# A linear-attention and FFT-convolution kernel: the filter loaded second, the angles in thirds, the last rows in merged transfers, and a new order of the work

## The chip, the cores and the metric

The kernel runs on one core of one Trainium2 chip. The metric is the device time of one execution in microseconds (us). Three runs of the kernel before gave a median of 219.78 us (219.63 to 219.86). One more execution was taken with the profiler.

## The reference: what is computed

For 8 batches, 8 heads, 576 positions and 64 values per head, all in float32:

```python
kv = np.einsum('bhsd,bhse->bhde', k, v)
out = np.einsum('bhsd,bhde->bhse', q, kv)
rms = np.sqrt(np.mean(out * out, axis=-1, keepdims=True) + 1e-06)
x = out / rms * g_norm            # heads put side by side: (8, 576, 512)
proj = x @ w_proj                 # x1, x2, x3: 512 columns each
X2, H = rfft(x2, axis=1), rfft(filter_fft, axis=0)
y = x1 * irfft(X2 * H, axis=1) * x3
return y @ w_out                  # (8, 576, 512)
```

## The kernel before, in words

**Stages of one batch.** The names are those of the steps in the table ORDER (L20); a step is written `name.batch`.

- Loads: `Lk`, `Lv`, `Lq` (whole or in halves a and b) fetch k, v, q as bf16 through POOL's DMA queue (L136 to L146). There are two buffers of each, so batch b overwrites batch b-2. `Lw1`, `Lw2`, `Lw3` fetch the three parts of w_proj, `Lwo` fetches w_out, `Lf` the filter.
- `K` multiplies k by v on PE (L377), `eK` copies the product to `kvblk`. q is transposed on PE (`T0`, `T1`, L416, copied by `eT..`) for batches 0 and 1 and by a DMA transpose on SP (`Qt`, L407) for the others; behind each `Qt` stands a small POOL copy (L408), which makes POOL wait for the transpose.
- `O` multiplies q by `kvblk` (L447); `sq` squares on ACT (L457); `R` sums on PE (L454); `rs` is the reciprocal root on ACT (L468); `ob` or `ov` copies the product (ACT or DVE); `x` multiplies both on DVE (L489).
- Gates: `Ga` and `Gb` (L631) are x by parts one and three of w_proj, 8 matmuls for each of four column blocks; `x1`/`xv` copies the one, `g` multiplies by the other on DVE (L639).
- The convolution: x is folded (`eo`, `fa`, `fr` on DVE), multiplied by part two of w_proj (`rrM`, `rrT`, `abM`, `abT`, L529 to L549), copied (`err`, `eab`, `eT`, L553), transformed (`F0`, `F1t`, `F1`, `F2c`, `F2`), multiplied by the filter's transform (`M0`, `M1`, `M2` on DVE, L606 and L621), summed (`A` on POOL or `Av` on DVE, L612), transformed back (`I`, `Io`, L661), copied to `ar` (`ea`, `oa` on ACT, `ev`, `ov` on DVE, L665), recombined on DVE (`vB`, `w`) and multiplied by the gates (`fin`, or `f0`, `f1` by halves, L683).
- Output: `U0`, `U2`, `U4` multiply by w_out (L716, L729) and `ot` copies and stores through SP's queue (L723, L736). The last batch has `V0` to `V3` (one bank each, L754), copies `va`/`vv` (L760), and stores `d..` of 32 rows each (L765): `dsCI` from SP, `dgCI` from POOL, `daCI` from ACT, for block group C and quarter I.

**The start.** Angles (`An`, L226) are made on DVE and turned to sines and cosines on ACT in one piece; PE transposes them into tables (`Tb0` to `Tb2`). The filter is folded (`Ff0` to `Ff2`, L315) and transformed (`H0` to `H2`, L332 and L335; copies L343 to L348).

**What sets the order.** ORDER is written by hand or by a search; each engine runs its instructions in the order in which the steps stand there, and waits for others through semaphores. A third number in a word (`T0.0.22`) puts that many filler matmuls on zeros (L112) ahead of the step. PSUM is four pairs of banks. `take` gives a step a pair, or one bank: before, one bank came from a pair with its other bank in use, if there was one. A transfer's end is counted by one of eight semaphore lanes for SP and ACT together (DMAHW0 to 7) and eight for POOL (DMASW0 to 7); a transfer waits for the one before it on its lane.

Of the kernel before, what the change touches and what calls it, by code (L numbers as in the profile page):

```python
# [19 lines left out]
ORDER = """Zi.0 Z.0 Zt.0 Lqa.0 Zd.0 An.0 Zf.0 Act.0 Lva.0 T0.0.22 eTv0.0 Tb1.0 Lka.0 Lvb.0 Tb2.0 Ka.0 eKva.0 Tb0.0 Lqb.0 O01.0.3  # L20
sq1.0 T1.0.3 R1.0.1 Lkb.0 ob1.0 eTv1.0 Lf.0 sq0.0 Kb.0 Lqa.1 eKvb.0 rs1.0 ov0.0 O23.0.4 R0.0 sq2.0 rs0.0 ov2.0 R2.0.2
sq3.0 ov3.0 Ff2.0 R3.0 rs3.0 rs2.0 Ff0.0 Lw1.0 Ff1.0 Lk.1 x.0 T0.1 eo.0 fr.0 eTv0.1 Lv.1 Lw3.0 Lqb.1 Ga0.0 Ga1.0 xv0.0
H0.0 H1.0 fa1.0 HN0.0 xv1.0 H2.0 K.1 Lw2.0 HN1.0 Lv.2 eK.1 Ga3.0 Gb1.0 fa0.0 T1.1 g1.0 eTa1.1 x13.0 Lkb.2 Gb3.0 rrM.0
rrT.0 g3.0 verr.0 O01.1 Lq.2 sq1.1 abM.0 F0.0 ov1.1 sq0.1 abT.0.1 ov0.1 eab.0 O23.1 F2c.0 eT.0 F2.0 sq2.1 M0.0 ob2.1
Gb0.0 M2.0 g0.0 sq3.1 F1t.0 Lka.2 Lqb.3 Lqa.3 A0.0 Qt.2 F1.0 ob3.1 R1.1 R3.1 Ga2.0 rs1.1 rs3.1 M1.0 R0.1 K.2 x12.0
rs0.1 R2.1 rs2.1 Gb2.0 Av1.0 eK.2 x.1 Io23.0 oa23.0 g2.0 Lk.3 I01.0 Io01.0 Lva.3 ea01.0 eo.1 I23.0 Lvb.3 O01.2 Lwo.0
oa01.0 Ga3.1 ea23.0 fa0.1 fa1.1 Qt.3 sq1.2 vB23.0 fr.1 ob1.2 Ga2.1 x13.1 sq0.2 x12.1 Lk.4 abM.1 ob0.2 eab.1 abT.1
O23.2 eT.1 vB01.0 sq2.2 w.0 ob2.2 rrM.1 rrT.1 F2c.1 Gb2.1 F2.1 err.1 fin.0 g2.1 sq3.2 Ga0.1 ob3.2 F0.1 x10.1 M2.1 R1.2
R2.2 rs1.2 Gb3.1 R3.2 rs2.2 F1t.1 F1.1 Lqa.4 Lq.5 M0.1 rs3.2 R0.2 K.3 g3.1 Ga1.1 rs0.2 M1.1 U0.0 eK.3 x11.1 x0.2 x1.2
Av1.1 ot0.0 O23.3 sq2.3 Gb0.1 g0.1 A0.1 ob2.3 eo.2 sq3.3 Gb1.1 I23.1 ob3.3 ea23.1 Ga0.2 Io23.1 g1.1 fa0.2 I01.1 x10.2  # L30
fa1.2 oa23.1 ev01.1 Io01.1 abT.2 O01.3 oa01.1 eT.2 fr.2 Lv.4 sq1.3 sq0.3 abM.2 ob1.3 eab.2 Ga3.2 vB.1 x13.2 rrM.2
ob0.3 R3.3 w.1 K.4 fin.1 F1t.2 rs3.3 F1.2 rrT.2 eK.4 Gb3.2 err.2 Lqb.4 M1.2 R0.3 rs0.3 Gb0.2 R2.3 Qt.4 g3.2 F0.2 g0.2
A1.2 R1.3 rs2.3 rs1.3 U4.1 Ga2.2 Ga1.2 x12.2 Qt.5 M0.2 x11.2 O23.4 F2c.2 x.3 F2.2 sq2.4 ob2.4 sq3.4 ob3.4 Lk.5 eo.3
U2.0 Gb1.2 fa.3 M2.2 U0.1 ot2.0 g1.2 Lk.6 R2.4 ot0.1 abT.3 Lva.5 Lq.6 eT.3 ov4r.1 Gb2.2 Av0.2 I01.2 rs2.4 Io23.2
Io01.2 g2.2 Lvb.5 ea01.2 I23.2 abM.3 oa23.2 fr.3 rrM.3 ev23.2 oa01.2 eab.3 vB.2 rrT.3 O01.4 w.2 F1t.3 err.3 sq1.4 F1.3
ob1.4 Lv.6 sq0.4 U2.1 ob0.4 Ga3.3 F0.3 M1.3 fin.2 A1.3 ot2.1 x13.3 R3.4 Ga2.3 rs3.4 M0.3 x12.3 Gb3.3 K.5 g3.3 eK.5
F2c.3 F2.3 R1.4 Gb2.3 R0.4 A0.3 rs1.4 M2.3 g2.3 I23.3 x1.4 rs0.4 ea23.3 I01.3 ea01.3 x0.4 eo.4 Ga0.3 O23.5 U0.2 sq3.5
ob3.5 xv0.3 fa0.4 sq2.5 ot0.2 ov2.5 fa1.4 Ga1.3 Io23.3 oa23.3 fr.4 Gb0.3 x11.3 abT.4 g0.3 Io01.3 veT.4 K.6 oa01.3
O01.5 eK.6 sq1.5 sq0.5 vB23.3 Gb1.3 ob1.5 vB01.3 abM.4 g1.3 ob0.5 rrM.4 rrT.4 eab.4 w.3 F1t.4 R1.5 Lk.7 f001.3 f101.3
err.4 f023.3 f123.3 R3.5 F1.4 Ga2.4 rs3.5 F0.4 rs1.5 R0.5 x12.4 M1.4 Ga1.4 R2.5 rs0.5 U2.2 x11.4 U4a.3 rs2.5 Qt.6 M0.4  # L40
O23.6 x.5 F2c.4 F2.4 ot2.2 M2.4 sq3.6 Gb1.4 ob3.6 g1.4 A1.4 sq2.6 U4b.3 Ga3.4 A0.4 ot4.3 ob2.6 I23.4 x13.4 eo.5 fr.5
Gb3.4 Io23.4 ea23.4 g3.4 Io01.4 oa23.4 vB23.4 w023.4 Ga0.4 I01.4 oa01.4 Gb2.4 ea01.4 g2.4 rrM.5 x10.4 w123.4 O01.6
rrT.5 sq1.6 vB01.4 U0.3 ov1.6 w001.4 err.5 Gb0.4 fa.5 abT.5 sq0.6 ot0.3 ob0.6 w101.4 R3.6 R2.6 g0.4 veT.5 rs3.6 F0.5
abM.5 rs2.6 Ga2.5 R1.6 f123.4 M0.5 f001.4 f023.4 Lv.7 Lq.7 eab.5 f101.4 x12.5 R0.6 rs0.6 Gb2.5 rs1.6 F1t.5 x1.6 K.7
F2c.5 F2.5 F1.5 Qt.7 A0.5 g2.5 U2.3 eK.7 M2.5 Ga3.5 ot2.3 O23.7 sq2.7 sq3.7 M1.5 xv3.5 Gb3.5 Ga0.5 Av1.5 ob3.7 g3.5
eo1.6 x0.6 eo0.6 x10.5 fa0.6 ob2.7 Ga1.5 Io01.5 Io23.5 I23.5 x11.5 oa23.5 Gb0.5 oa01.5 I01.5 ea01.5 fa1.6 abM.6 ea23.5
U0.4 g0.5 vB01.5 abT.6 fr0.6 eab.6 vB23.5 w001.5 ot0.4 w101.5 Gb1.5 fr1.6 O01.7 eT.6 w023.5 sq0.7 g1.5 ob0.7 F1t.6
w123.5 F1.6 Ga3.6 x13.6 rrM.6 F2c.6 M1.6 sq1.7 rrT.6 R3.7 ob1.7 F2.6 Gb3.6 err.6 rs3.7 fin.5 A1.6 M2.6 g3.6 Ga0.6 F0.6
Ga1.6 R1.7 x10.6 x11.6 Gb1.6 M0.6 rs1.7 Gb0.6 R0.7 Ga2.6 g1.6 R2.7 rs0.7 U0.5 g0.6 A0.6 x0.7 rs2.7 x1.7 xv2.6 I23.6
ot0.5 ea23.6 I01.6 eo.7 Ga1.7 Io01.6 ea01.6 oa01.6 Gb2.6 x11.7 Io23.6 fa.7 oa23.6 abM.7 g2.6 Ga0.7 fr.7 abT.7 eab.7  # L50
eT.7 x10.7 rrM.7 rrT.7 F2c.7 F1t.7 vB.6 F2.7 w.6 F1.7 U2.5 err.7 fin.6 M2.7 M1.7 A1.7 F0.7 ot2.5 M0.7 U0.6 Gb0.7 ot0.6
U2.4 Av0.7 g0.7 Gb1.7 I23.7 ot2.4 I01.7 g1.7 ea01.7 U4a.5 U4b.5 ea23.7 Io01.7 Io23.7 oa01.7 vB01.7 oa23.7 vB23.7 Ga2.7
w001.7 f001.7 Gb2.7 Ga3.7 ot4.5 Gb3.7 x12.7 x13.7 g2.7 g3.7 U2.6 w023.7 f023.7 U4a.7 w123.7 U4b.7 w101.7 ot2.6 va4.7
V0.7 da42.7 da40.7 dg41.7 f101.7 f123.7 dg43.7 V3.7 va3.7 da32.7 vv0.7 V1.7 dg03.7 ds30.7 V2.7 da33.7 da00.7 vv1.7
vv2.7 ds11.7 dg31.7 da02.7 ds13.7 dg01.7 ds23.7 dg12.7 dg10.7 dg22.7 da20.7 da21.7"""
# [3 lines left out]
def kernel(  # L59
# [165 lines left out]
    @one  # L225
    def An(b):  # L226

        ang = work.tile([P, 2, 3, TH], FP32, name="ang", tag="tpw1")
        a_, r_ = ang[:, 0], ang[:, 1]
        for c in range(3):  # L230
            vec.tensor_scalar_mul(out=a_[:, c], in0=tmp['tv'], scalar1=kcol[:, c:c + 1])
        vec.tensor_scalar(out=r_, in0=a_, scalar1=0.5 / S, scalar2=MAGIC, op0=ALU.mult, op1=ALU.add)
        vec.tensor_scalar(out=r_, in0=r_, scalar1=MAGIC, scalar2=-2.0 * S, op0=ALU.subtract, op1=ALU.mult)
        vec.tensor_tensor(out=r_, in0=r_, in1=a_, op=ALU.add)
        act.activation(out=IV[:, 1:6:2], in_=r_, func=AF.Sin, scale=W0)
        act.activation(out=a_, in_=r_, func=AF.Abs)
        for h, n in ((0, 2), (1, 1)):
            act.activation(out=IV[:, 4 * h:4 * h + 2 * n - 1:2], in_=a_[:, 2 * h:2 * h + n], func=AF.Sin, scale=cosb[:, 2 + h:3 + h], bias=cosb[:, h:h + 1])
# [228 lines left out]
    def e_rs(b, j):  # L467
        act.activation(out=halves(rstd()[:, j]), in_=tmp['r', b, j][:, :, 0:TH], func=AF.Abs_reciprocal_sqrt, scale=1.0 / D, bias=bias_eps)  # L468
# [294 lines left out]
    def V_out(b, key, i, q):  # L763
        rows = o_rows(b - 1 + i // 2, (NB - 2, NB - 1, 0, 1)[i]) if key == 4 else o_rows(b, 2 * (b % 2) + 4 * key + i)
        q.dma_start(out=rows, in_=tmp['ot', b, key][32 * i:32 * i + 32])  # L765
# [51 lines left out]
```

## Time and profile before

| what | value |
|---|---|
| median of three runs | 219.78 us |
| the profiled execution's own time | 221.13 us |
| its span | 219.3 us |
| PE, DVE, ACT, POOL busy | 92%, 84%, 67%, 30% |
| instructions | 4987 |
| filler matmuls asked for in ORDER | 36 |
| HBM read, written | 33.69 MB, 9.44 MB |

PE is TensorE's matmuls and PEld its weight loads, DVE is VectorE, ACT ScalarE, POOL GpSimd, SP SyncE; a q behind a name is the engine's queue, in which DMA issues and waits are seen. Rows of instructions give the start, the length, the engine, the line, what is written from what, how many, and in brackets the idle time before them with what ended it. Rows of groups give busy time and mean ns, then idle time and what ended it. Line numbers are those of the kernel before.

### The profile page before, as it was taken

To read this page: it belongs to the slowest core of one execution; us is meant where nothing else is said; L and a number is where in the kernel's file an instruction comes from. 1 tells how busy PE (TensorE), PEld (TensorE's weight loads), DVE (VectorE), ACT (ScalarE), POOL (GpSimd) and SP (SyncE) were. 2 spreads that over 40 slices of the span, in tenths; PEclk is the share of its full clock that TensorE was granted. 3 is DMA by queue.
4 is the path that set the end of the run, shared out by engine and by line. 5 is a ranking of instruction groups with operands and counts; after the bars stand their busy time and mean duration, and the time that the engine had idled before them with its cause. 6 is when DMAs were issued, how large, how long until landed. Compare 5 with 4: busy or idle time off the path is not lost.

```text
span 219.3 us, 4987 instructions
## 1 busy us (share of the span) xinstructions
PE 200.9 (92%) x2017; PEld 120.7 (55%) x2041; DVE 184.4 (84%) x284; ACT 146.8 (67%) x227; POOL 66.0 (30%) x72
## 2 busy tenths in 40 slices
...
GB/s 48 165 214 200 208 205 206 204 208 162 208 202 147 166 135 83 137 241 257 243 111 138 73 4 160 198 152 54 96 0 99 0 6 94 0 193 111 13 184 175
DMA packets 37146, 30.16 MB, mean 137 GB/s; under 512 B 16162, under 2 KB 32546, under 8 KB 37122
## 3 DMA queue, kind: packets, MB, share of 16 engines
...
q1 hardware_dynamic: 19394, 11.93, 23.4%
q10 hardware_dynamic: 384, 0.52, 0.9%
...
HBM read 33.69 MB, written 9.44 MB: 197 GB/s over the span
## 4 chain that ended last, share of the span: by engine, by line
PE 79%; DVE 6%; ACT 5%; issue 4%; POOL 2%; POOLq 0%; DVEq 0%; ACTq 0%
PE ps L631 27%; PE ps L716 11%; PE ps L543 6%; PE ps L661 4%; PE ps L454 4%; PE ps L529 3%; PE ps L549 3%; PE ps L377 2%; PE ps L447 2%; PE ps L536 2%; PE ps L587 2%; PE ps L573 2%; POOL out_dram L765 2%; PE ps L332 1%; PE ps L112 1%
## 5 line engine op out<-in xcount | busy, mean ns | idle before, releaser
L631 PE MATMUL ps<-x,wp 128*128 128x288 bf16 x512 | 71.2, 286 | 0.4 <-DVE HH L348 0.2
L631 PEld LDWEIGHTS <-wp 128*128 128x128 bf16 x512 | 48.9, 98 | 18.2 <-issue 2.5
L612 POOL TENSOR_TENSOR Y<-tpw 97x1024 bf16<-97x1024 f32 (+1 forms) x11 | 29.1, 2648 | 64.4 <-DVE tpw L606 64.3
L606 DVE TENSOR_TENSOR tpw<-ps,HH 97x2048 f32<-97x2048 f32 (+1 forms) x16 | 36.4, 2288 | 2.5 <-PE ps L587 1.3
L639 DVE TENSOR_TENSOR g<-ps,x 128x576 bf16<-128x576 f32 x32 | 24.0, 752 | 4.2 <-PE ps L631 2.2
L468 ACT ACTIVATE rstd<-ps,bias_eps 128x576 bf16<-128x576 f32 x32 | 23.1, 742 | 5.6 <-PE ps L454 5.4
L716 PE MATMUL ps<-wo,yg 128*128 128x512 bf16 x107 | 26.2, 379 | 0.4 <-ACT x L637 0.2
L553 ACT CAST x<-ps 128x1024 bf16<-128x1024 f32 (+1 forms) x21 | 18.6, 893 | 8.4 <-PE ps L543 4.7
L457 ACT ACTIVATE sq<-ps 128x576 bf16<-128x576 f32 x32 | 20.7, 659 | 4.7 <-PE ps L447 4.6
L720 ACT COPY ot<-ps 128x1024 f32<-128x1024 f32 x14 | 14.2, 1017 | 13.8 <-PE ps L716 12.1
L637 ACT CAST x<-ps 128x576 bf16<-128x576 f32 x27 | 17.5, 647 | 7.5 <-PE ps L631 5.6
L665 ACT CAST ar<-ps 128x576 bf16<-128x576 f32 x30 | 18.1, 645 | 6.4 <-PE ps L662 6.2
L464 ACT ACTIVATE o<-ps,g_col 128x576 bf16<-128x576 f32 x25 | 18.7, 753 | 0.0
L408 POOL COPY one__101<-qT 1x2 bf16<-1x2 bf16 x6 | 4.0, 670 | 46.7 <-DMA qT<-qb 46.7
L716 PEld LDWEIGHTS <-yg 128*128 128x128 bf16 x112 | 10.8, 98 | 12.3 <-issue 0.9
L661 PE MATMUL ps<-IV,Y 128*128 128x192 bf16 x128 | 15.9, 245 | 0.1
L543 PE MATMUL ps<-wp,ab 128*128 128x512 bf16 x59 | 14.9, 379 | 0.3
L662 PE MATMUL ps<-IV,Y 97*128 97x96 bf16 x64 | 13.2, 207 | 1.4 <-DVE Y L612 1.4
L140 POOL DMA_DIRECT2D qb<-in_q_dram x12 | 8.9, 745 | 12.6 <-PE ps L416 9.9
L454 PE MATMUL ps<-sq,ind 128*128 128x288 bf16 x64 | 12.3, 286 | 0.2 <-issue 0.2
L112 PE MATMUL ps<-nil,ind 128*128 128x512 bf16 x34 | 10.7, 441 | 2.0 <-DVE ind L193 1.6
L489 DVE TENSOR_TENSOR x<-o,rstd 128x1152 bf16<-128x1152 bf16 (+1 forms) x12 | 11.9, 1008 | 0.6 <-ACT rstd L468 0.6
...
## 6 DMA issues: line engine op xcount, KB each, us to landing
...
vb<-in_v_dram POOLq DMA_DIRECT2D x5, 576.0 KB, 17.2
...
kb<-in_k_dram POOLq DMA_DIRECT2D x4, 288.0 KB, 13.6
```

The source lines that it names most:

```text
L454: nc.tensor.matmul(r2[:, h, 0:TH], ind, sq()[:, j, h * TH:(h + 1) * TH], start=True, stop=True)
L457: act.activation(out=halves(sq()[:, j]), in_=tmp['o', b, j][:, :, 0:TH], func=AF.Square)
L464: act.activation(out=halves(osb()[:, j]), in_=i_, func=AF.Copy, scale=g_col)
L468: act.activation(out=halves(rstd()[:, j]), in_=tmp['r', b, j][:, :, 0:TH], func=AF.Abs_reciprocal_sqrt, scale=1.0 / D, bias=bias_eps)
L543: nc.tensor.matmul(pp[:, h], abt()[:, j, 2 * h * P:(2 * h + 1) * P], w2(j), start=(j == 0), stop=(j == NDC - 1))
L553: act.copy(out=o_(), in_=tmp[key, b])
L606: vec.tensor_mul(out=t_[:n], in0=xp[:n].unsqueeze(1).to_broadcast([n, 2, 2, DM]), in1=two)
L612: op(out=Yt()[:n, 2 * g:2 * g + 2], in0=t_[:n, ::-1, 0], in1=t_[:n, ::-1, 1])
L631: nc.tensor.matmul(pp[:, h, 0:TH], w_, x[:, j, h * TH:(h + 1) * TH], start=(j == 0), stop=(j == NDC - 1))
L639: vec.tensor_mul(out=halves(g13t()[:, dc]), in0=pp[:, :, 0:TH], in1=x1)
L661: nc.tensor.matmul(pp[:, i, 0:SB], Y[:, 2 * g + h, cs], IV[:, 2 * g + h, 0:SB], start=(g == 1), stop=(g == 2))
L716: nc.tensor.matmul(pp[:, cc], ygt(b)[:, dc, b % 2 * 64 + c * P:b % 2 * 64 + (c + 1) * P], wo[:, dc], start=(dc == 0), stop=(dc == NDC - 1))
```

## The change

1. **Loads.** The filter (`Lf`) stands second, behind the first half of q and ahead of the rest of batch 0; `Lw3` now precedes `Lw1`. Whole loads of q are mostly split into halves.
2. **Filter.** Folding and the first part of its transform (`H1`) come ahead of batch 0's O, `H0` and `H2` ahead of its gates. The folded filter lies in the output buffer yg instead of the work buffer that the angles use.
3. **Angles** are made in thirds (`An2`, `An1`, `An0`): three DVE operations and three ACT operations each.
4. **`take`**: one bank comes from a half-used pair only if no pair is free.
5. **Last rows**: each block of the last batch is stored by two transfers instead of four, over 1 to 3 groups of 32 rows; ACT issues none of them.
6. **`Qh`**: the POOL copy is a step of its own and stands behind every second transpose.
7. `rs` has its small bias as an immediate value.
8. **ORDER** is written anew: 37 fillers, five more `ar` copies on DVE, ten sums on POOL instead of eleven.

The loads at the start of POOL's queue, before; `qb`, `vb`, `kb` are q, v, k with buffer numbers (74, 72, 70 for batch 0; 75 for q of batch 1), `fn` is the filter, `wp` w_proj:

```order
L140 DMA qb_74<-in_q_dram 96x4x384
L144 DMA vb_72<-in_v_dram 128x2x576
L144 DMA kb_70<-in_k_dram 128x2x576
L144 DMA vb_72<-in_v_dram 128x2x576
L140 DMA qb_74<-in_q_dram 96x4x384
L144 DMA kb_70<-in_k_dram 128x2x576
L301 DMA fn<-in_moe_filter_fft_dram 96x3072
L140 DMA qb_75<-in_q_dram 96x4x384
L152 DMA wp<-in_moe_w_proj_dram 128x4x512
```

And after:

```order
L140 DMA qb_74<-in_q_dram 96x4x384
L307 DMA fn<-in_moe_filter_fft_dram 96x3072
L140 DMA qb_74<-in_q_dram 96x4x384
L144 DMA vb_72<-in_v_dram 128x2x576
L144 DMA kb_70<-in_k_dram 128x2x576
L144 DMA vb_72<-in_v_dram 128x2x576
L144 DMA kb_70<-in_k_dram 128x2x576
L152 DMA wp<-in_moe_w_proj_dram 128x4x512
```

The filter has moved ahead of five transfers of batch 0, and the first part of w_proj ahead of batch 1's q.

ACT's queue behind the tables, before; `ff` is the folded filter and `hu` a copy of its transform, `sq` and `rstd` belong to batch 0's norm:

```order
L457 ACTIVATE sq<-ps_68 128x576
L464 ACTIVATE o<-ps_68,g_col 128x576
L457 ACTIVATE sq<-ps_67 128x576
L468 ACTIVATE rstd<-ps_66,bias_eps 128x576
L457 ACTIVATE sq<-ps_69 128x576
L468 ACTIVATE rstd<-ps_66,bias_eps 128x576
L457 ACTIVATE sq<-ps_68 128x576
L468 ACTIVATE rstd<-ps_69,bias_eps 128x576
L468 ACTIVATE rstd<-ps_67,bias_eps 128x576
L317 CAST ff<-ps_68 128x1024
L317 CAST ff<-ps_66 128x1024
L343 ACTIVATE hu<-ps_66,cf 97x1024
```

And after, where the folded filter is written to `yg`:

```order
L323 CAST yg<-ps_67 128x1024
L323 CAST yg<-ps_68 128x1024
L429 COPY qT<-ps_69 128x1152
L349 ACTIVATE hu<-ps_68,cf 128x1024
L466 ACTIVATE sq<-ps_67 128x576
L466 ACTIVATE sq<-ps_66 128x576
L389 CAST kvblk_78<-ps_69 128x2x64
L389 CAST kvblk_78<-ps_69 64x2x64 x2
L466 ACTIVATE sq<-ps_69 128x576
L466 ACTIVATE sq<-ps_68 128x576
L477 ACTIVATE rstd<-ps_66 128x576
```

The filter's copies have moved from behind the norm to ahead of it, with one of the three transform copies and the copy of K's second half between them.

The end of SP's queue, before, with the semaphores that each issue waits for; `ot` holds output blocks, `vb`, `kb`, `sq` serve as output buffers of the last batch:

```order
L723 DMA out_dram<-ot 32x2x512 [waits DMAHW2_49]
L723 DMA out_dram<-ot 32x2x512 [waits DMAHW4_49]
L736 DMA out_dram<-ot 32x512 [waits DMAHW7_49,Activation_49]
L736 DMA out_dram<-ot 32x512 [waits DMAHW1_49]
L736 DMA out_dram<-ot 32x512 [waits DMAHW3_49]
L736 DMA out_dram<-ot 32x512 [waits DMAHW5_49]
L723 DMA out_dram<-ot 32x2x512 [waits DMAHW7_49,Activation_49]
L723 DMA out_dram<-ot 32x2x512 [waits DMAHW0_49]
L723 DMA out_dram<-ot 32x2x512 [waits DMAHW1_49]
L723 DMA out_dram<-ot 32x2x512 [waits DMAHW2_49]
L765 DMA out_dram<-vb_73 32x512 [waits DMASW7_49,DMAHW3_49,DMASW4_49,Activation_49]
L765 DMA out_dram<-kb_71 32x512 [waits DMAHW4_49,DMASW3_49,DVE_49]
```

And after:

```order
L732 DMA out_dram<-ot 32x2x512 [waits DMAHW7_49,Activation_49]
L732 DMA out_dram<-ot 32x2x512 [waits DMAHW0_49]
L732 DMA out_dram<-ot 32x2x512 [waits DMAHW1_49]
L732 DMA out_dram<-ot 32x2x512 [waits DMAHW2_49]
L781 DMA out_dram<-vb_72 2x32x512 [waits DMAHW3_49,DMASW4_49,Activation_49]
L781 DMA out_dram<-kb_71 32x512 [waits DMAHW4_49,DMASW7_49,DVE_49]
L781 DMA out_dram<-kb_71 3x32x512 [waits DMAHW5_49]
L781 DMA out_dram<-vb_73 32x512 [waits DMAHW6_49,DMASW6_49]
L781 DMA out_dram<-sq 2x32x512 [waits DMAHW7_49,DVE_49]
L781 DMA out_dram<-sq 2x32x512 [waits DMAHW0_49]
L781 DMA out_dram<-kb_70 3x32x512 [waits DMAHW1_49,DMASW5_49,Activation_49]
```

The lanes follow each other by one now, since SP alone uses them there, and five of the last seven issues carry two or three groups of 32 rows, listed with the group as outermost dimension.

The diff, cut; of ORDER its first and last lines:

```diff
-ORDER = """Zi.0 Z.0 Zt.0 Lqa.0 Zd.0 An.0 Zf.0 Act.0 Lva.0 T0.0.22 eTv0.0 Tb1.0 Lka.0 Lvb.0 Tb2.0 Ka.0 eKva.0 Tb0.0 Lqb.0 O01.0.3
+ORDER = """Z.0 Lqa.0 Zi.0 Lf.0 Zt.0 An2.0 An1.0 An0.0 Zd.0 Act.0 Zf.0 Zr.0 T0.0.18 Tb2.0 Lqb.0 Tb0.0 eTv0.0 Lva.0 Tb1.0.3 Ff0.0
...
-vv2.7 ds11.7 dg31.7 da02.7 ds13.7 dg01.7 ds23.7 dg12.7 dg10.7 dg22.7 da20.7 da21.7"""
+ds10.7 U4b.7 dg21.7 V0b.7 vv4.7 va0.7 ds30.7 dg00.7 ds40.7 ds41.7 ds01.7"""
...
-        if n == 1 and odd:
+        if n == 1 and odd and all(max(seen[2 * i], seen[2 * i + 1]) >= TAKEN for i in range(4)):
...
+        vec.tensor_scalar_mul(out=kturn, in0=kcol, scalar1=0.5 / S)
...
+    def angles(c):
+
+        if 'ang' not in tmp:
+            tmp['ang'] = work.tile([P, 2, 3, TH], FP32, name="ang", tag="tpw1")
+        a_, r_ = (tmp['ang'][:, i, c] for i in range(2))
+        h = c // 2
+        vec.tensor_scalar(out=a_, in0=tmp['tv'], scalar1=kturn[:, c:c + 1], scalar2=MAGIC, op0=ALU.mult, op1=ALU.add)
+        vec.tensor_scalar(out=r_, in0=a_, scalar1=MAGIC, scalar2=-2.0 * S, op0=ALU.subtract, op1=ALU.mult)
+        vec.scalar_tensor_tensor(out=a_, in0=tmp['tv'], scalar=kcol[:, c:c + 1], in1=r_, op0=ALU.mult, op1=ALU.add)
+        act.activation(out=IV[:, 2 * c + 1], in_=a_, func=AF.Sin, scale=W0)
+        act.activation(out=r_, in_=a_, func=AF.Abs)
+        act.activation(out=IV[:, 2 * c], in_=r_, func=AF.Sin, scale=cosb[:, 2 + h:3 + h], bias=cosb[:, h:h + 1])
...
-            tmp['ff'] = work.tile([P, 3, 2, DM], BF16, name="ff", tag="tpw1")
+            tmp['ff'] = yg4().rearrange("p a j s -> p (a j s)")[:, 0:6 * DM].rearrange("p (a i d) -> p a i d", a=3, i=2)
...
+    @one
+    def Qh(b):
         nc.gpsimd.tensor_copy(out=one_, in_=qT(b)[0:1, 0, 0:2])
...
-        act.activation(out=halves(rstd()[:, j]), in_=tmp['r', b, j][:, :, 0:TH], func=AF.Abs_reciprocal_sqrt, scale=1.0 / D, bias=bias_eps)
+        act.activation(out=halves(rstd()[:, j]), in_=tmp['r', b, j][:, :, 0:TH], func=AF.Abs_reciprocal_sqrt, scale=1.0 / D, bias=1e-6)
...
     def V_out(b, key, i, q):
-        rows = o_rows(b - 1 + i // 2, (NB - 2, NB - 1, 0, 1)[i]) if key == 4 else o_rows(b, 2 * (b % 2) + 4 * key + i)
-        q.dma_start(out=rows, in_=tmp['ot', b, key][32 * i:32 * i + 32])
+        if key == 4:
+            bb, blk, i0, n = b - 1 + i, (NB - 2, 0)[i], 2 * i, 2
+        else:
+            x0 = 2 * (b % 2) + 4 * key
+            cut = 3 - x0 % 3 if x0 % 3 else 3
+            i0, n = ((0, cut), (cut, 4 - cut))[i]
+            bb, blk = b, x0 + i0
+        rows = bass.AP(tensor=out.tensor, offset=out.offset + (bb * S + t_of(blk)) * DM, ap=[[2 * DM, n], [6 * DM, 32], [1, DM]])
+        q.dma_start(out=rows, in_=tmp['ot', b, key][32 * i0:32 * (i0 + n)])
...
-        for i in range(4):
+        for i in range(2):
             for e, q_ in (("s", nc.sync), ("g", nc.gpsimd), ("a", nc.scalar)):
                 step["d%s%d%d" % (e, c, i)] = lambda b, c=c, i=i, q_=q_: V_out(b, c, i, q_)
```

90 lines of the change are left out of this document (41 added, 49 removed).

## The prediction

> **What bounds the kernel now.** I read the page first, then the stretches, the timelines of PE, SP and the copies, the waits and the DMA view.
>
> ```profile
> span 219.3 us, 4987 instructions
> PE 200.9 (92%) x2017; PEld 120.7 (55%) x2041; DVE 184.4 (84%) x284; ACT 146.8 (67%) x227; POOL 66.0 (30%) x72
> 40.00:50.00 10.00, 9.16 (x141) 5.74 (x141) 9.20 (x7) 8.20 (x14) 4.04 (x4) 1.00 1.23 207
> 205.00:210.00 5.00, 4.17 (x20) 1.67 (x18) 1.67 (x5) 1.97 (x3) 1.06 (x2) 1.00 0.25 54
> 210.00:215.00 5.00, 0.00 (x0) 0.00 (x0) 1.62 (x3) 0.00 (x0) 2.95 (x6) 0.76 0.81 222
> 215.00:219.30 4.30, 0.00 (x0) 0.00 (x0) 0.00 (x0) 0.00 (x0) 0.00 (x0) 0.50 0.51 153
> ```
>
> In the stretches the columns after the length are PE, PEld, DVE, ACT, POOL, then clock, DMA share and GB/s. PE is busy for 92% of the span, so the middle is PE's, with DVE close behind. After 209.2 PE does nothing: the last 10 us belong to transfers. Time can come from three places: PE's start, PE's stalls in the middle, and the end.
>
> The end first, by PE's and SP's timelines and SP's waits:
>
> ```profile
> 205.55 3.62 PE L754 MATMUL ps<-wo,yg 128*128 128x512 bf16 x16
> 200.56 11.25 SPq L736 DMA_DIRECT2D out_dram<-ot  x4
> 211.91 2.95 SPq L723 DMA_DIRECT2D out_dram<-ot  x4
> 216.70 0.36 SPq L765 DMA_DIRECT2D out_dram<-vb  x1
> SPq L736 <- DMA out_dram<-sq: 9.0, 2, 8.7
> ```
>
> The last matmul ends at 205.55 + 3.62 = 209.17; the span ends 10.15 us later. SP stood for 8.7 us in one L736 issue, since its semaphore lane was held by a row transfer that ACT issues late, and the 512 KB of batch 6 left only at 211.91. The last issue is at 216.70.
>
> **The end, part by part.** The changed order issues nothing from ACT there, so SP's lanes follow each other and that wait goes. What is late next is the merged transfer itself. V_out now lists the rows as 3 or 2 blocks x 32 rows, with the block dimension outermost, against 96 or 64 partitions. One transfer of the old kernel has such a short outermost dimension: g_col, listed as 2 x 64 against 128 partitions. The DMA view from 0 to 5 us, where g_col is SP's only transfer; ACT's queue on the page (each row packets, MB, share); and the costs beside them:
>
> ```profile
> q1 hardware_dynamic: 130, 0.00, 1.1%
> q10 hardware_dynamic: 384, 0.52, 0.9%
> g_col<-in_g_norm_dram SPq DMA_DIRECT2D x1, 0.5 KB
> L199 SPq DMA_DIRECT2D g_col<-in_g_norm_dram x1: 724/724/724, 0.7 to 0.7; - x1
> out_dram<-kb SPq DMA_DIRECT2D x2, 64.0 KB, 2.1
> 216.80:217.10 0.30, 0.00 (x0) 0.00 (x0) 0.00 (x0) 0.00 (x0) 0.00 (x0) 0.50 0.58 191
> ```
>
> ACT's queue carried 8 transfers of 32 rows: 384 = 8 x (32 + 16), one closing packet from each of 16 engines. g_col left 130 = 128 + 2: two engines. I take a merged transfer to run on 3 or 2 engines, so each of them carries 32 rows of 2 KB, 65.5 KB, where the old 32-row transfer gives each engine two rows.
>
> [...]
>
> Price of one: the load stretch 40 to 50 moves 207 GB/s of bf16 out of twice that in fp32, 414 / 16 = 25.9 GB/s an engine, so 2.5 us; the stretch 216.8 to 217.1 moves 191 / 16 / 0.58 = 20.6 GB/s per busy engine, so 3.2 us. I take 2.7, nearer the fast row, since a narrow transfer has its engine almost alone. SP issues five of them (one of V2, V1, V0 each, two of U4), between two wide ones. On the same engines they run one after the other: 13.5 us (12.5 to 16), and 0.4 for the wide ones' rows.
>
> When the first starts, from the rows of the copies:
>
> ```profile
> 202.41 1.58 DVE L639 TENSOR_TENSOR g<-ps,x 128x576 bf16<-128x576 f32 x2
> 205.62 0.83 DVE L683 TENSOR_TENSOR yg<-w,g 128x576 bf16<-128x576 bf16 x2
> 205.80 0.59 ACT L760 COPY sq<-ps 128x512 f32<-128x512 f32 x1
> ```
>
> After the last gate (call its end t) DVE needs 0.79 for g2 and 0.42 for the product, so with the semaphores between them V3's second half starts at about t+1.4; V3 and V2 are done by t+2.5, their two copies on ACT by t+3.3. PE has 20 matmuls of 0.22 behind the gate (3.62 / 16) and waits about 0.75 for DVE: it ends at t+5.05. So the first narrow issue stands at T - 1.65, T being the last matmul's end. A wide 64 KB lands 2.1 after its issue, 0.2 of it data, so 1.9 is fixed; before, the end came 219.3 - (216.70 + 2.1) = 0.5 after the last landing. End = T - 1.65 + 1.9 + 13.5 + 0.4 + 0.5 = T + 14.65, against T + 10.15: **+4.5** (+3.5 to +7.0). PE's wait of 0.75 stands for one of some 0.35 between the last rows of before: **+0.4**. POOL's two narrow transfers go beside these; on the same engines each would add 2.7, which the upper end covers.
>
> **The start.** PE's rows, of which everything useful counts:
>
> ```profile
> 24.08 2.12 PE L631 MATMUL ps<-x,wp 128*128 128x288 bf16 x16
> 31.29 0.78 PE L377 MATMUL ps<-vb,kb 64*64 64x64 bf16 x72
> 36.27 1.03 PE L529 MATMUL ps<-wp,rr 128*128 128x512 bf16 x3
> 38.15 1.90 PE L543 MATMUL ps<-wp,ab 128*128 128x512 bf16 x8
> L152 POOL DMA_DIRECT2D wp<-in_moe_w_proj_dram x1: 747/747/747, 15.4 to 15.4; - x1
> DMA to landing us min/median/max: 18.8/18.8/18.8
> ```
>
> Before, the first gate runs at 24.08 and the filter's transform from 26.2 to 31.29, 5.1 us; in the new order that is done before the first gate. So the same work would stand at 24.08 + 5.1 = 29.2, and a first gate earlier than that is gain. The chain to it:
>
> ```profile
> 6.84 0.92 ACT L235 ACTIVATE IV<-ang 128x864 bf16<-128x864 f32 x1 [3.52 <-DVE ang L234]
> 8.61 1.39 ACT L238 ACTIVATE IV<-ang,cosb 128x576 bf16<-128x576 f32 x2
> L343 ACT ACTIVATE hu<-ps,cf 97x1024 f32<-97x1024 f32 (+1 forms) x2 | 2.2, 1114 | 4.0 <-PE ps L332 4.0
> L383 ACT CAST kvblk<-ps 64x256 bf16<-64x256 f32 (+1 forms) x21 | 7.7, 369 | 1.8 <-PE ps L377 1.5
> L457 ACT ACTIVATE sq<-ps 128x576 bf16<-128x576 f32 x32 | 20.7, 659 | 4.7 <-PE ps L447 4.6
> L468 ACT ACTIVATE rstd<-ps,bias_eps 128x576 bf16<-128x576 f32 x32 | 23.1, 742 | 5.6 <-PE ps L454 5.4
> L317 DVE CAST ff<-ps 32x1024 bf16<-32x1024 f32 x1 | 1.2, 1201 | 0.0
> ```
>
> ACT's angles take 6.84 to 10.0 in one piece behind 3.5 us of DVE; by thirds ACT starts after one, at about 4.5, and needs 1.3 a third: 8.4. Transposes and fillers bring PE to 11.0, DVE's copies of tables end, by my estimate from their number, at about 14.6, that of the third fold 1.2 later, 15.8. Then one after the other: V-K product and the transform's first part to 17.2, its copy 1.1, two squares 1.3, the second half's K copies 1.1 (behind the fillers, to 20.9), O23 with two more squares 1.8, four rstd 3.0: 25.7. PE does H0 and H2 from 24.7 to 27.9, when the first gate starts: 1.3 ahead of 29.2. Followed on to abM with the same five gates, K, T1, rrM, rrT and O01 behind it, I get 36.2 where 38.15 stands: **-2.0**. More is not to be had: the weights of rrM land at 15.4 + 18.8 = 34.2, behind the same set of loads in both orders, and rrM stood at 36.27. The bound on the other side is 0: the fillers may run short or ACT, which now carries the filter's copy between K and the squares, be late by as much. Range -3.0 to 0. The filter's earlier load moves batch 0's by some 2.8 us, which the table chain covers by 1 to 2 us.
>
> **The middle.** PE's waits between 34 and 205, and DVE's copies and sums that grow in number:
>
> ```profile
> PE ps L662 <- DVE Y L612: 1.4, 1, 1.4
> PE ps L598 <- ACT x L553: 0.7, 1, 0.7
> L665 DVE CAST ar<-ps 128x576 bf16<-128x576 f32 x2 | 1.5, 754 | 0.1
> L612 DVE TENSOR_TENSOR Y<-tpw 128x1024 bf16<-128x1024 f32 (+1 forms) x5 | 6.2, 1232 | 0.1
> L462 DVE TENSOR_SCALAR o<-ps,g_col 128x576 bf16<-128x576 f32 x7 | 5.6, 812 | 0.6 <-ACT sq L457 0.6
> ```
>
> The first wait comes of batch 2's sum on DVE behind an output copy; both are elsewhere in the new order. The second comes of eT waiting for F2c in the other bank of its pair; a free pair takes that away. That is 2.1 us at most. Against it DVE gets about 3 us more in all (five ar of 0.75, an o of 0.81, one Y sum of 1.2, less three x copies of about the ar's 0.75 and an output copy), and an order written anew has stalls that no row of before shows. I take **-0.6**, with -2.0 to +1.5. Qh for every second transpose frees POOL, which is idle most of the time: 0. The immediate bias in rstd: 0, since neither its shape nor its engine changes; a gain or loss of some hundredths on each of 32 lies inside the bounds.
>
> **The sum.** +4.5 + 0.4 - 2.0 - 0.6 = +2.3 on the span of 219.3, which gives 221.6; the profiled execution took 221.13 and the median of the runs is 219.78, so 219.78 + 2.3 = **222.1**. With the bounds together (not all at one end) the case has 220.0 to 225.4.
>
> **The rivals.**
> - *Narrow, but on different engines each time*: the transfers run side by side. The last is issued six issues later (four at 0.72, as g_col, two at 0.33): T - 1.65 + 3.5 = T + 1.9; it lands 1.9 + 2.7 later, and 0.5 ends it: T + 7.0, -3.15 instead of +4.5. Total -5.4: 214.4. For it: nothing in the trace ties a transfer to particular engines. [...] Chance 0.11.
> - *Full width*: the merged transfers use 16 engines as the old ones did. The last copy ends 0.7 after T, a landing 2.1 and three blocks' data 0.8 follow, some queueing, 0.5: T + 4.6, -5.55. Total -7.8: 212.0. This is the change doing all it can; it decides if packets close with 16 each. Against: g_col's 130. Chance 0.13.
>
> What the new order gains ahead of the end is part of my case, 0.76: from 4.9 us there on, the longer end is paid for.
>
> **Chances.** About 0.2% (0.4 us) is what a measurement of this kernel can tell from none. Of my 0.76, 0.61 lies above that, 0.05 within, 0.10 below; the rivals are all below. Faster 0.34, same 0.05, slower 0.61. For 8 in 10 the range reaches down to the first rival: 214.0 to 225.4; the likeliest case alone has 220.0 to 225.4.
>
> **What would show it.** Right: after the last matmul some 14 to 15 us, SP's last issue soon after T with landings stretched to 10 us and more, and a DMA share of 0.1 to 0.2 there at 60 to 80 GB/s; the first gate at 28, abM near 36. Wrong: landings near 2 us at the end and 200 GB/s and more, or the end at T + 5 to T + 7; or PE's waits in the middle growing past 3 us.

## The result, and the profile after

| | before | changed |
|---|---|---|
| median | 219.82 us | 228.1 us |
| ratio to before, 95% interval | | 1.0377 [1.0345, 1.0409] |
| the profiled execution, its span | 221.13, 219.3 | 227.85, 226.1 |
| last matmul ends (call it T) | 209.17 | 206.43 |
| from T to the end of the span | 10.15 | 19.67 |

The changed kernel is slower by 8.3 us. The sign was forecast, the size was not: 222.1 was said, 225.4 at most. By the two profiled executions the span is longer by 6.8 us: 2.74 gained ahead of T, 9.52 lost behind it. Two executions on record ran far longer at a lower granted clock, one of e4 (257.71 us, clock 0.823) and one of the kernel before (345.1 us, 0.563), and the ratios leave them out.

Two lines of the page of the changed kernel, then rows of its PE and SP timelines (start, length, engine, line, operation, count):

```profile
span 226.1 us, 5000 instructions
PE 202.1 (89%) x2042; PEld 119.9 (53%) x2042; DVE 183.6 (81%) x283; ACT 146.9 (65%) x235; POOL 59.2 (26%) x65
```

```profile
28.81 3.11 PE L640 MATMUL ps<-x,wp 128*128 128x288 bf16 x24
37.10 1.90 PE L552 MATMUL ps<-wp,ab 128*128 128x512 bf16 x8
204.55 0.60 SPq L781 DMA_DIRECT2D out_dram<-vb  x1
205.84 0.59 PE L763 MATMUL ps<-wo,yg 128*128 128x512 bf16 x2
212.04 2.02 SPq L781 DMA_DIRECT2D out_dram<-kb  x1
```

The first gate and abM are the two rows at the top. SP begins its last rows 1.88 us ahead of T = 205.84 + 0.59 and issues the last of them at 212.04, where before the last issue stood at 216.70. So SP no longer stands for 9 us in one wait, as forecast. What follows is transfers alone. The stretches of the changed kernel (after the length PE, PEld, DVE, ACT, POOL, then clock, DMA share, GB/s), and, from the DMA view of 205 to 226 us, the landings of some transfers (KB each, us from issue to landing) and the row of SP's queue (packets, MB, share):

```profile
206.00:208.00 2.00, 0.43 (x3) 0.00 (x0) 0.69 (x1) 0.58 (x1) 0.53 (x1) 1.00 0.58 67
210.00:212.00 2.00, 0.00 (x0) 0.00 (x0) 0.00 (x0) 0.00 (x0) 0.00 (x0) 0.81 0.60 127
216.00:218.00 2.00, 0.00 (x0) 0.00 (x0) 0.00 (x0) 0.00 (x0) 0.00 (x0) 0.50 0.20 75
218.00:220.00 2.00, 0.00 (x0) 0.00 (x0) 0.00 (x0) 0.00 (x0) 0.00 (x0) 0.50 0.14 54
220.00:222.00 2.00, 0.00 (x0) 0.00 (x0) 0.00 (x0) 0.00 (x0) 0.00 (x0) 0.50 0.13 51
222.00:224.00 2.00, 0.00 (x0) 0.00 (x0) 0.00 (x0) 0.00 (x0) 0.00 (x0) 0.50 0.09 37
```

```profile
out_dram<-vb POOLq DMA_DIRECT2D x1, 192.0 KB, 8.0
out_dram<-kb SPq DMA_DIRECT2D x1, 64.0 KB, 9.1
out_dram<-vb SPq DMA_DIRECT2D x1, 64.0 KB, 9.7
q1 hardware_dynamic: 492, 0.92, 15.3%
```

A DMA share of 0.13 is two of 16 engines, 0.20 is three; they move 51 and 75 GB/s, 25 each. SP's 492 packets are 448 rows of 2 KB and 44 of 4 bytes that close, 2 x 16 for the two transfers of 64 KB and 3 x 2 + 2 x 3 for the merged ones. So the merged transfers are as narrow as forecast. The two of 64 KB, which close with 16 packets each, land 9.1 and 9.7 us after their issue where two such landed in 2.1 before; rows that stand behind merged ones would explain it.

### The profile page after: what moved, and what is told of

Read it like the earlier page. It is cut to its first block, busy times and chain, and to the rows that moved or that the text cites. A ratio compares the mean times of both kernels' runs of the same rounds, so it can differ in the third digit from the quotient of the medians.

```text
span 226.1 us, 5000 instructions
## 1 busy us (share of the span) xinstructions
PE 202.1 (89%) x2042; PEld 119.9 (53%) x2042; DVE 183.6 (81%) x283; ACT 146.9 (65%) x235; POOL 59.2 (26%) x65
## 4 chain that ended last, share of the span: by engine, by line
PE 63%; issue 15%; DVE 5%; ACT 4%; POOL 3%; POOLq 0%; DVEq 0%; ACTq 0%
PE ps L640 21%; PE ps L725 7%; PE ps L552 6%; PE ps L670 4%; PE ps L463 3%; PE ps L456 3%; POOL Y L621 3%; PE ps L538 2%; PE ps L558 2%; PE ps L383 2%; DVE tpw L615 2%; PE ps L338 2%; PE ps L545 1%; PE ps L112 1%; PE ps L596 1%
## 5 line engine op out<-in xcount | busy, mean ns | idle before, releaser
L621 POOL TENSOR_TENSOR Y<-tpw 128x1024 bf16<-128x1024 f32 (+1 forms) x10 | 25.9, 2594 | 105.5 <-DVE tpw L615 105.5
L646 ACT CAST x<-ps 128x576 bf16<-128x576 f32 x30 | 19.0, 643 | 11.4 <-PE ps L640 9.7
L729 ACT COPY ot<-ps 128x1024 f32<-128x1024 f32 x14 | 14.2, 1014 | 12.4 <-PE ps L725 12.3
L477 ACT ACTIVATE rstd<-ps 128x576 bf16<-128x576 f32 x32 | 20.1, 652 | 2.7 <-PE ps L463 2.4
L466 ACT ACTIVATE sq<-ps 128x576 bf16<-128x576 f32 x32 | 20.0, 653 | 2.2 <-PE ps L456 2.0
L674 ACT CAST ar<-ps 128x576 bf16<-128x576 f32 x25 | 15.1, 645 | 7.7 <-PE ps L671 6.8
L473 ACT ACTIVATE o<-ps,g_col 128x576 bf16<-128x576 f32 x24 | 17.7, 749 | 0.0
L140 POOL DMA_DIRECT2D qb<-in_q_dram x15 | 10.5, 702 | 13.8 <-PE ps L425 12.0
L112 PE MATMUL ps<-nil,ind 128*128 128x512 bf16 x37 | 11.9, 458 | 1.6 <-DVE ind L194 1.6
L510 DVE TENSOR_TENSOR eo<-x 128x576 bf16<-128x576 bf16 (+1 forms) x26 | 12.1, 522 | 0.1
L498 DVE TENSOR_TENSOR x<-o,rstd 128x1152 bf16<-128x1152 bf16 (+1 forms) x11 | 11.2, 1029 | 1.0 <-ACT rstd L477 1.0
```

Of the source, the lines that this page charges most:

```text
L466: act.activation(out=halves(sq()[:, j]), in_=tmp['o', b, j][:, :, 0:TH], func=AF.Square)
L621: op(out=Yt()[:n, 2 * g:2 * g + 2], in0=t_[:n, ::-1, 0], in1=t_[:n, ::-1, 1])
L646: ev0(out=x1, in_=pp[:, :, 0:TH])
```

## The experiments

Each compares with the kernel before on the same chip, 220.1 to 220.2 us there. To set ends side by side, times after T are taken from each kernel's own profile: that cancels what happened ahead of T in that one execution. In this code the merged transfers of batch 7 are, in SP's order, 128 KB (two blocks), 192 (three), 128, 128, 192, with two of 64 KB between, and from GpSimd 192, 128 and one of 64.

**e1: the last rows as before, in 32-row transfers.** Everything else of the change stays.

```diff
-q.dma_start(out=rows, in_=tmp['ot', b, key][32 * i0:32 * (i0 + n)])
+for x in range(n):
+    q.dma_start(out=o_rows(bb, blk + x), in_=tmp['ot', b, key][32 * (i0 + x):32 * (i0 + x) + 32])
```

> The changed kernel with its last rows stored in transfers of 32 rows again (two or three issues where one stood, same queue, same place); nothing else is undone. Theory N (a merged transfer runs on 2 or 3 engines, and always the same ones): the end shrinks from 19.7 us behind the last matmul to 4 to 6, so 212 to 214 us. Rival Q (SP's many issues in the new order are what takes the time, whatever their width): no gain or some us more, 226 to 231. The gain ahead of the last matmul (2.7 us) stays in both.

Measured: 215.47 us, ratio 0.9786 [0.9769, 0.9803]. That is 1.5 us above theory N's range and far below rival Q's, and this version beats both kernels. PE, SP and the stretches of e1:

```profile
205.81 0.59 PE L763 MATMUL ps<-wo,yg 128*128 128x512 bf16 x2
209.76 1.31 SPq L781 DMA_DIRECT2D out_dram<-kb  x3
206.00:208.00 2.00, 0.41 (x2) 0.00 (x0) 0.69 (x1) 0.58 (x1) 1.33 (x3) 1.00 0.92 273
210.00:212.00 2.00, 0.00 (x0) 0.00 (x0) 0.00 (x0) 0.00 (x0) 0.00 (x0) 0.93 0.50 133
out_dram<-kb SPq DMA_DIRECT2D x7, 64.0 KB, 1.8
```

Nothing ahead of T moved (206.40), the end comes 7.3 us after it instead of 19.67, and 64 KB land in 1.8 us. So the merged transfers cost 12.4 us by the profiles, and by the ratios (1.0377 - 0.9786) x 220 = 13.0.

**e2: only GpSimd's merged transfers split again.**

```diff
+if q is nc.gpsimd:
+    for x in range(n):
+        q.dma_start(out=o_rows(bb, blk + x), in_=tmp['ot', b, key][32 * (i0 + x):32 * (i0 + x) + 32])
+    return
```

> The changed kernel with only POOL's merged transfers split into 32 rows each; SP's five stay merged. Theory N with POOL's two on the same engines as SP's: their 2 x 2.6 us leave the chain, 228.1 - 5.2 = 223 us. Rival P (a narrow transfer costs 3.7 us, POOL's run elsewhere): SP's five still take 18 us, 227.5 to 228.5.

Measured: 226.84 us, 1.031 [1.0282, 1.0337], between the two figures; the end comes at T + 18.6. Two transfers fewer in the chain should have given 5 us and gave 1.3. My explanation of the missing 5 us by GpSimd's transfers seemed to fall; e5, e6, e13 and e14 show what of it stands.

**e3: three of SP's merged transfers issued by ACT.**

```diff
-ds10.7 ... ds40.7 ds41.7 ds01.7
+da10.7 ... da40.7 da41.7 ds01.7
```

> The changed kernel with three of SP's five merged transfers (of V1 and U4) issued by ACT, still merged. Theory N (the same engines, whatever queue issues): no gain, 226 to 230 us. Rival S (one queue works off its transfers one after the other, each on engines of its own): the two queues run side by side, some 5 to 7 us less, 221 to 223.

Measured in a single execution: 227.93 us, span 226.2, T + 19.7, as with SP alone. Issuing three of them from ACT's queue brings no other engines into play here: by the DMA view the last ones move 75 to 78, then 50 to 53 GB/s, as in the changed kernel (75, then 51 to 54). The packets of the trace (what an engine moves at a time, here a row of 2 KB) show it too: from 216 to 220 us a row of SP's and a row of ACT's follow each other in turn, in two runs side by side.

**e4: the merge put into the kernel before**, nothing else of the change: seven merged transfers, four of them from ACT, two from SP, one from GpSimd.

```diff
-q.dma_start(out=rows, in_=tmp['ot', b, key][32 * i:32 * i + 32])
...
+rows = bass.AP(tensor=out.tensor, offset=out.offset + (bb * S + t_of(blk)) * DM, ap=[[2 * DM, n], [6 * DM, 32], [1, DM]])
+q.dma_start(out=rows, in_=tmp['ot', b, key][32 * i0:32 * (i0 + n)])
```

> The kernel before with only the last rows merged as in the change (two transfers a block, each from the queue and place of its first old issue). Theory N: seven narrow transfers of 2.6 us one behind the other from 206.4 on, an end near 227 and 227 to 230 us in all. Rival O (the new order's end is what costs, the merge is harmless): within 1 us of 219.8.

Measured: 236.14 us (the median of three of its four executions), 1.0732 [1.0697, 1.0766], so 16.1 us, more than both expectations. The merge alone makes the old kernel slower by more than the whole change does. Why it costs more here than the 12 to 13 us of e1 stays open: the one trace kept of e4 is that of the 257.71 us execution.

**e5: the changed kernel without GpSimd's three transfers.**

```diff
+if q is nc.gpsimd:
+    return
```

> The changed kernel without GpSimd's three last-row transfers (192 + 128 KB merged and one 64 KB): those rows of batch 7 are not written. SP's five merged ones stay. Theory S (all merged transfers of whatever queue share the same two or three engines, 2.7 us each; with GpSimd's two that is 7 x 2.7 = 18.9 instead of 13.5, and T + 20.05 beside the 19.67 seen): the end falls to T + 14.7, so 222.7 to 223.3 us. Rival C (SP's chain alone costs 3.5 to 3.7 us a transfer and GpSimd's have nothing to do with it, as making them wide, -1.3 us, seemed to show): 226.0 to 227.5.

Measured: 225.51 us, 1.0257 [1.0226, 1.0289], which lies between the two theories: 2.6 us less than the changed kernel. In the profile SP's chain stands alone (SP's first merged issue, the last matmuls, stretches):

```profile
204.60 0.60 SPq L783 DMA_DIRECT2D out_dram<-vb  x1
205.89 0.59 PE L763 MATMUL ps<-wo,yg 128*128 128x512 bf16 x2
206.00:208.00 2.00, 0.48 (x3) 0.00 (x0) 0.69 (x1) 0.59 (x1) 0.00 (x0) 1.00 0.39 59
210.00:212.00 2.00, 0.00 (x0) 0.00 (x0) 0.00 (x0) 0.00 (x0) 0.00 (x0) 0.79 0.20 77
216.00:218.00 2.00, 0.00 (x0) 0.00 (x0) 0.00 (x0) 0.00 (x0) 0.00 (x0) 0.50 0.13 50
218.00:220.00 2.00, 0.00 (x0) 0.00 (x0) 0.00 (x0) 0.00 (x0) 0.00 (x0) 0.50 0.13 51
```

Two engines move 50.5 GB/s, so one moves 25.3, and its 65.5 KB take 2.59 us. The span is 223.3: T + 16.8. From the first issue to the end are 18.7 us; five times 2.59 are 12.95, and 5.75 are left for the start, the two transfers of 64 KB and the closing.

**e6: GpSimd's rows issued by ACT, full width**, SP's chain as it is.

```diff
+if q is nc.gpsimd:
+    for x in range(n):
+        nc.scalar.dma_start(out=o_rows(bb, blk + x), in_=tmp['ot', b, key][32 * (i0 + x):32 * (i0 + x) + 32])
+    return
```

> The changed kernel with GpSimd's three last-row transfers issued by ACT as six full-width ones of 64 KB; SP's five merged ones stay. Theory G (GpSimd's queue is what held the shared engines even with wide transfers: its packets there took 0.2 to 1.0 us each): the six then cost each engine 12 rows x 0.084 = 1.0 us, and the time is 223.0 to 224.5. Rival W (any transfers beside the chain cost it as much, whatever queue): 226.3 to 227.5, as with GpSimd's wide ones (226.8).

Measured: 225.79 us, 1.0255 [1.0231, 1.0278], between the two figures; theory G's was built on e5's lower expectation. By the profiles, one execution each, the end comes at T + 16.8 without these rows (e5), T + 17.7 with ACT's full-width ones (e6), T + 18.6 with GpSimd's full-width ones (e2) and T + 19.67 with GpSimd's merged ones. So ACT's cost 0.9 us, near the 1.0 of theory G, and GpSimd's 0.9 more. The ratios give nothing for ACT's (1.0255 against e5's 1.0257) and 0.0055 x 220 = 1.2 us between e2 and e6, with intervals that just part. Executions of one of these kernels differ by 1 us or so, which makes this step weaker than the others; if it holds, it is why e2 gained so little. The landings of e2, then of e6, go the same way:

```profile
out_dram<-vb POOLq DMA_DIRECT2D x5, 64.0 KB, 5.1
out_dram<-vb ACTq DMA_DIRECT2D x5, 64.0 KB, 2.7
```

Why GpSimd's full-width rows hold the chain up more, no run shows.

**e7 and e10: e1 with only SP's last transfer merged, and with its last two.**

```diff
+if not ((key, i) in ((0, 1),)):              # e10: ((4, 1), (0, 1))
+    for x in range(n):
+        q.dma_start(out=o_rows(bb, blk + x), in_=tmp['ot', b, key][32 * (i0 + x):32 * (i0 + x) + 32])
+    return
```

> All last rows by full-width 32-row transfers except the very last one, 96 rows in one merged transfer. Price of a merged transfer by itself, beside 215.5 us with none. Theory S (2.7 us of data, two issues of 0.44 fewer): 215.5 + 2.5 - 0.9 = 217.1, 216.5 to 217.5. Rival C (3.5 to 3.7 us by itself): 217.9 to 218.3. If merged transfers ran at full width: 214.6 to 215.0.

> All last rows by full-width transfers but SP's last two (128 KB and 192 KB), merged. With only the last one merged the time was 218.4 and the end came 10.25 us behind the last matmul. Theory L (a chain of merged transfers pays a slow first stretch once, then 2.56 us of rows each): + 2.56 - 0.44 (one issue fewer ahead) = +2.1, 220.5 us, T + 12.4. Rival C (each merged transfer costs 3.7 to 4.1 us): +3.3 to +3.7, 221.7 to 222.1, T + 13.5 to 14.

Measured: e7 218.43 us, 0.9925 [0.9909, 0.9942]; e10 220.26 us, 1.0009 [0.9995, 1.0023]. The first merged transfer costs 3.1 us over e1 and ends above both expectations. The second costs 1.8 more, near theory L's 2.1 and far from rival C's 3.3 to 3.7. PE's and SP's last rows, then stretches, of e7:

```profile
207.25 0.59 PE L763 MATMUL ps<-wo,yg 128*128 128x512 bf16 x2
211.21 0.82 SPq L785 DMA_DIRECT2D out_dram<-kb  x1
212.00:213.00 1.00, 0.00 (x0) 0.00 (x0) 0.00 (x0) 0.00 (x0) 0.00 (x0) 0.74 0.07 14
213.00:214.00 1.00, 0.00 (x0) 0.00 (x0) 0.00 (x0) 0.00 (x0) 0.00 (x0) 0.50 0.21 25
214.00:215.00 1.00, 0.00 (x0) 0.00 (x0) 0.00 (x0) 0.00 (x0) 0.00 (x0) 0.50 0.16 49
215.00:216.00 1.00, 0.00 (x0) 0.00 (x0) 0.00 (x0) 0.00 (x0) 0.00 (x0) 0.50 0.19 74
```

And of e10:

```profile
205.83 0.59 PE L763 MATMUL ps<-wo,yg 128*128 128x512 bf16 x2
208.78 0.60 SPq L785 DMA_DIRECT2D out_dram<-sq  x1
```

In e7 three engines hold the one transfer, and for two microseconds they move 14 and 25 GB/s, then 49, and only then 74. From the issue at 211.21 to the end of the span at 218.1 are 6.9 us, 2.59 of them rows: 4.3 fixed. Packet by packet, 1.4 us pass before the first merged row, the rows take 4.1 instead of 2.59, and 1.3 follow the last; the slow rows are the early ones, up to 0.84 us each where the later ones take 0.084. In e10 (span 218.5) 9.7 - 2 x 2.59 = 4.5. So e10's chain of two pays the slow first stretch once, and then 2.59 or less for each transfer.

**e8: e1 with rstd's bias from the tile, as before.**

```diff
-... scale=1.0 / D, bias=1e-6)
+... scale=1.0 / D, bias=bias_eps)
```

> Last rows by full-width 32-row transfers, and rstd's bias read from the tile of 1e-6 as before instead of the immediate; nothing else changed. ACT's rstd should go back from 652 to 742 ns, 2.9 us of ACT in all. Theory I (the immediate carries part of the 2.7 us that the kernel gained ahead of the end, since TensorE waits for rstd through the x copies): 216.5 to 218.0 beside 215.5. Rival O (ACT is off the path nearly everywhere; the new order carries the gain): 215.3 to 215.9.

Measured: 215.77 us, 0.9807 [0.9792, 0.9821], whose interval overlaps e1's. The group of rstd in e8, then in e1:

```profile
L477 ACT ACTIVATE rstd<-ps,bias_eps 128x576 bf16<-128x576 f32 x32 | 22.9, 743 | 2.6 <-PE ps L463 2.3
```

```profile
L477 ACT ACTIVATE rstd<-ps 128x576 bf16<-128x576 f32 x32 | 20.1, 652 | 2.7 <-PE ps L463 2.4
```

The immediate frees 91 ns of ACT 32 times, 2.8 us in all. The kernel's gain is 0.0021 x 220 = 0.5 us by the ratios, which the intervals do not tell from none: rival O.

**e9: e1 with only GpSimd's transfers merged.**

```diff
+if not (q is nc.gpsimd):
+    for x in range(n):
+        q.dma_start(out=o_rows(bb, blk + x), in_=tmp['ot', b, key][32 * (i0 + x):32 * (i0 + x) + 32])
+    return
```

> All of SP's last rows by full-width 32-row transfers; GpSimd's 192 and 128 KB stay merged. Theory S (GpSimd's merged transfers also have two or three engines only, and the low ones that SP's share): the 192 KB land some 7 us after the issue and the 128 KB later still, the end comes behind them, 216 to 218 us beside 215.5 with none merged. Rival D (GpSimd's queue deals a merged transfer to other engines or to all of them): landings of 2.2 to 4 us, 215.2 to 215.8 us.

Measured: 218.24 us, 0.9912 [0.9885, 0.9939], just above theory S's range and 2.8 us above e1; the end comes at T + 10.0. Landings in e9:

```profile
out_dram<-kb SPq DMA_DIRECT2D x7, 64.0 KB, 5.7
out_dram<-vb POOLq DMA_DIRECT2D x1, 192.0 KB, 6.6
out_dram<-vb POOLq DMA_DIRECT2D x1, 128.0 KB, 7.2
```

GpSimd's merged transfers land in 6.6 and 7.2 us, its 64 KB ones in e1 in 2.2, which fits narrow ones; SP's full-width ones, which land in 1.8 us in e1, now take 5.7, which fits rows that stand behind the merged ones.

**e13 and e14: which engines GpSimd's take.** All other last rows are left out. In e13 only GpSimd's 192 and 128 KB are written, in e14 GpSimd's 192 KB and SP's first 192 KB.

```diff
+if (key, i) not in ((3, 1), (2, 1)):         # e14: ((3, 1), (1, 0))
+    return
```

> Of batch 7's last rows only GpSimd's two merged transfers (192 and 128 KB) are written; all other last rows are left out, so nothing else is in the engines. Theory S (GpSimd's queue gives a merged transfer two or three engines as SP's does): once the earlier output is gone the data move at 75 to 78 GB/s with three engines and 50 to 52 with two, 160 KB of 320 of them at the least, and the landings are 6 to 8 us. Rival D (dealt to more engines): over 120 GB/s, landings under 4 us.

> Of batch 7's last rows only one merged transfer of 192 KB from GpSimd and one of 192 KB from SP are written, all others left out. Theory S (the same three engines for both): together 77 GB/s or less while both move, and the later one lands some 2.6 us later than it would alone. Rival O (GpSimd's lie on three other engines; what they cost beside SP's chain in the changed kernel is then something else): up to 150 GB/s together, and about 7 us for each from issue to landing.

One execution each: 214.69 and 217.15 us. Stretches of e13, then SP's issue and stretches of e14:

```profile
208.00:209.00 1.00, 0.00 (x0) 0.00 (x0) 0.00 (x0) 0.00 (x0) 0.00 (x0) 1.00 0.33 91
209.00:210.00 1.00, 0.00 (x0) 0.00 (x0) 0.00 (x0) 0.00 (x0) 0.00 (x0) 1.00 0.28 95
```

```profile
205.53 0.82 SPq L783 DMA_DIRECT2D out_dram<-kb  x1
209.00:210.00 1.00, 0.00 (x0) 0.00 (x0) 0.00 (x0) 0.00 (x0) 0.00 (x0) 1.00 0.16 47
211.00:212.00 1.00, 0.00 (x0) 0.00 (x0) 0.00 (x0) 0.00 (x0) 0.00 (x0) 0.50 0.20 78
212.00:213.00 1.00, 0.00 (x0) 0.00 (x0) 0.00 (x0) 0.00 (x0) 0.00 (x0) 0.50 0.13 51
```

In e13, 91 and 95 GB/s are more than the 77 of three engines and less than the 120 of rival D: the two transfers do not lie on the same three, yet neither uses all. The packets, 4 KB each from GpSimd, form five runs side by side from 208.3 to 208.9 us: three engines and two others. In e14 the two together move more than 78 GB/s, three engines' worth, in no microsecond, and SP's needs 215.4 - 205.53 = 9.9 us to the end where in e7 it needed 6.9: they share, and SP's pays 3.0 for GpSimd's 2.6. Here too the packets agree: SP's three runs of rows begin at 209.16, 209.92 and 211.34, each within 5 ns of the end of one of GpSimd's three. In the changed kernel itself GpSimd's packets and SP's rows follow each other in turn, in three runs between 207 and 212 us. So in these traces the three-block one of GpSimd's two sits on the engines of SP's chain and the other on others. What decides on which engines a transfer lies, and their numbers, no run here shows.

**e11: e1 with four transfers from ACT instead of SP.**

```diff
-ds40.7 ds41.7 ds01.7
+da40.7 da41.7 ds01.7
```

> All last rows by full-width transfers, and the four of the two-batch tile issued by ACT instead of SP. Theory P (with wide transfers SP's issues of 0.44 one after the other set the end): SP's last issue ends 1.7 to 2.0 us earlier and the end with it, 213.3 to 214.2 us beside 215.5. Rival E (the engines' data is the limit there, or ACT waits for a lane as in the kernel before): 215.3 to 217.

Measured: 216.06 us, 0.9811 [0.9782, 0.984], no gain. A row of SP in e11:

```profile
205.62 4.23 SPq L781 DMA_DIRECT2D out_dram<-kb  x4
```

The four issues that took 1.72 us in e1 take 4.23: what ACT took over, SP lost in a wait of 2.6 us for `out_dram<-sq`, which ACT issues there. The time is rival E's; the wait that rival E gave ACT is SP's.

**e12: e1 with the old rule for single banks.**

```diff
-if n == 1 and odd and all(max(seen[2 * i], seen[2 * i + 1]) >= TAKEN for i in range(4)):
+if n == 1 and odd:
```

> Last rows by full-width transfers, and a single bank again taken from a half-used pair whenever there is one. Theory B (the rule of the free pair took away a wait of 0.7 us, at most 2): 216.0 to 217.0 us beside 215.5, with a wait of PE for ACT's x copies back. Rival N (in the new order the rule decides nothing that is waited for): 215.2 to 215.8.

Measured: 217.67 us, 0.9885 [0.9857, 0.9914], 2.2 us above e1, where theory B had 2 at most. abM still starts at 37.09. PE's waits between 34 and 209 us in e12, and its last matmuls:

```profile
PE ps L763 <- DVE kb L769: 0.8, 1, 0.8
PE ps L590 <- ACT x L562: 0.7, 1, 0.7
PE ps L596 <- issue: 0.5, 3, 0.2
PE ps L607 <- ACT ot L742: 0.3, 1, 0.3
208.35 0.59 PE L763 MATMUL ps<-wo,yg 128*128 128x512 bf16 x2
```

The wait of 0.7 for ACT's x copies is back, as expected, but it is only a third of the price. Beside it stand 0.8 for DVE's copy `kb` in the last rows, 0.3 for ACT's `ot`, and small ones; which of these come of a shared pair the rows don't say. The same view of the changed kernel, from 34 to 206 us, holds a single row:

```profile
PE ps L763 <- DVE yg L692: 0.6, 1, 0.6
```

## Why the prediction was right in sign and too small

**The end: the chain was right, its term too small.** The forecast failed at the term End = T + 14.65: the end came at T + 19.67, beyond even the upper bound of +7.0, which is T + 17.15. The prediction said that a merged transfer runs on three or two engines and that those of one queue follow each other there. Shares of 0.20 and 0.13 show the first, e3, e7 and e10 the second, and e1 what the merge costs: 12.4 to 13.0 us. That the five would stand on the same engines, which makes them 13.5 us in the sum, no row of before shows; it was my assumption. In e5, with SP's five alone, the share from 210 us on is 0.20 at most, three engines, and in e10 the same. The price of one, 2.7, was nearly right (2.59). The 5.0 us by which T + 14.65 was short come from these places:

- *The fixed part.* I gave a chain the 1.9 + 0.5 us of a wide transfer. e7 and e10 measured 4.3 and 4.5. In e5 the chain of five left 5.75, where 2.8 had been counted with 0.4 for the wide ones: **2.95 too little**, 0.9 of it beyond what e7 and e10 show and unexplained. The row behind the 1.9 was that of a 64 KB transfer, which closes with 16 packets; for a chain of transfers that close with two or three there was no row, and I took the near one without a bound above.
- *GpSimd's transfers* were named and priced at nothing, with 2.7 each in the upper end. Without them the end comes at T + 16.8 (e5) instead of T + 19.67: **2.85** by the profiles, 2.6 by the medians, one transfer's worth; e13 and e14 show why it is one and not two. This is a failure of the assumed overlap and not of a price: that GpSimd's would run beside SP's chain had no row behind it, and half of it was so.
- *The transfer and the start* gave 0.55 and 0.23 back: 5 x (2.7 - 2.59), and the first issue 1.88 ahead of T instead of 1.65. The 1.65 was a slip: 20 x 3.62 / 16 + 0.75 is 5.27 and not 5.05, which would have given 1.87. 2.95 + 2.85 - 0.55 - 0.23 = 5.0.

**The start: half of it came.** abM stands at 37.10, 1.05 earlier, where 2.0 was said; the first gate at 28.81 instead of 27.9. ACT's last row of the angles in the changed kernel:

```profile
8.93 0.63 ACT L238 ACTIVATE IV<-ang,cosb 128x288 bf16<-128x288 f32 x1
```

They end at 9.56, 0.4 earlier than before and not 1.6. ACT did start early, at 5.25 instead of the 4.5 estimated, and needed 1.4 a third instead of 1.3; each small error lay on the chain. No run undid the thirds, so this is read from the rows alone.

**The middle: more came.** From abM to T the kernel needs 169.33 us where it needed 171.02: 1.69 less, against 0.6 less 0.4. The bound of 2.1 for both waits was the better figure. e12 gives the bank rule alone 2.2 us in the new order; the new stalls that I set against it did not come (the single row above). That the gain ahead of T came near its forecast, 2.74 against 2.2, is luck: the start fell short by 0.95 and the middle went beyond by 1.5.

**The base.** Terms were worked on the profiled execution and laid on the median. That of before lay 1.3 above its median, that of the changed kernel 0.25 below. So 6.8 us of span became 8.3 of median: 1.5 of the 6.0 that the forecast missed is this, and no mechanism is known for it. The other 4.5 are 5.0 at the end and 0.95 at the start, less 1.5 in the middle.

**The rivals.** "Full width" is refuted by the DMA shares of 0.13 and 0.20. Its 212.0 was never tried, and the terms it lists make T + 4.1, not T + 4.6, unless the 0.5 that ends the span is added. With 32-row transfers e1 reaches 215.5; SP issues 14 of them there one after the other, the last ending at 211.07, T + 4.7. "On different engines each time" is refuted for SP and ACT by e3 and for SP by e10.
